# Turning the tokens of seven experts with VectorE blocks in place of TensorE transposes, in a fused attention and mixture-of-experts kernel

## The chip, the core and the metric

The kernel runs on one core of one Trainium2 chip. The metric is the device time of one launch in microseconds. The kernel before takes 764.63 us (median of 3 runs, 764.2 to 764.87).

## The reference

Bucketed attention over 4 batches of 8 heads, 768 tokens each, width 64, feeds a mixture of 8 experts that takes one expert per token:

```
mask   = q_bucket[:, :, :, None] == k_bucket[:, :, None, :]
attn   = softmax(where(mask, scale * q @ k.T, -1e9))
x      = (attn @ v).transpose(0, 2, 1, 3).reshape(3072, 512)
expert = argmax(x @ w_gate); gate_w = softmax(x @ w_gate)[expert]
for e in range(8):                      # tokens sorted by expert
    h = maximum(x_sorted[lo:hi] @ w1[e], 0)       # 512 -> 1024
    y_sorted[lo:hi] = h @ w2[e]                   # 1024 -> 512
out = gate_w * y (in the tokens' own order)
```

## The kernel before

The first 455 us or so are attention. Its results are scattered as rows of 578 floats into a table in device memory, `sorted_rows`, one stretch per expert: eight heads' 64 values with gate columns between them, then the gate weight and the token's number. The change does not touch that part, nor the first expert, which is taken in two halves of 256 tokens.

The rest is nine phases (`PH`). Phases 0 and 1 are the two halves of the fullest expert. Phases 2 to 8 are the seven others, in order of their fill, with room for 456, 432, 408, 396, 384, 372 and 354 tokens (`CAPS`). Phases 2 to 5 so have four row tiles of up to 128 tokens, phases 6 to 8 three.

In phase n, `mm1` (L697) makes the hidden values, 1024 of them in 8 groups of 128, each group 12 matmuls that move the tokens `xh` (feature on the partition, token along the free axis). Numbers are held as a rounded high part and a low part (a product is high x high and the two mixed ones), so the 4 chunks of 128 features need 3 matmuls each. ScalarE writes the high part of the relu (L711), VectorE the low part (L713). `mm2` makes the output: for phases of more than 384 tokens with features on the partitions (L734, 4 groups of 24), evicted as `yt` by ScalarE (L738) and turned back during the next phase's `mm1` (L763); for phases of up to 384 tokens by token (`yout`, L754, one group of 24 per row tile). VectorE applies the gate (L765), GpSimd scatters the rows (L767).

The tokens of phase n+1 are fetched by `rows(n + 1)` at the start of phase n: one DMA per row tile on SP's queue, 128 whole rows (L639, tile `xg`). During `mm2` of phase n they are turned by `xt` (L659): TensorE transposes each 128x128 block against an identity matrix into PSUM, ScalarE writes the high part of `xh` (L664), VectorE the low part (L665). A written table, `XT`, says behind or in the middle of which group of `mm2` each of the four chunks is turned. The gate weights and token numbers are copied by L662 and L645.

Weights: SP loads `raw` half chunks (L611), ScalarE writes the high part (L624), GpSimd the low part (L625), one phase ahead of their use, into six buffers; `halves` spreads those pieces over the groups of `mm1` and `mm2`. Each engine runs its instructions in the order in which they are written.

Of the kernel before, what the change touches and what calls it, by code (L numbers as in the profile page):

```python
# [7 lines left out]
F32 = mybir.dt.float32  # L8
F32R = mybir.dt.float32r
BF16 = mybir.dt.bfloat16  # L10
I32 = mybir.dt.int32
AF = mybir.ActivationFunctionType
OP = mybir.AluOpType
AX = mybir.AxisListType

B, H, S, D = 4, 8, 768, 64
# [5 lines left out]
DM = H * D  # L22
N = B * S
E = 8
F = 1024
PW = 2 * (D + E)
GC = NP * PW
RW = GC + 2
# [10 lines left out]
EARLY = 256  # L39
CAPS = [512, 456, 432, 408, 396, 384, 372, 354]  # L40
# [7 lines left out]
def tiles_of(n):  # L48

    return [(o, min(128, n - o)) for o in range(0, n, 128)]  # L50


@with_exitstack
def lsh_attention_moe(ctx, tc, qk, qk2, v, proj, wg, w1, w2, out):
    nc = tc.nc
    const = ctx.enter_context(tc.tile_pool(name="const", bufs=1))
    moe = ctx.enter_context(tc.tile_pool(name="moe", bufs=1))
# [3 lines left out]
    wk = attn.enter_context(tc.tile_pool(name="wk", bufs=2))  # L61
# [399 lines left out]
    EV = {}  # L461
# [133 lines left out]
    P2 = {}  # L595

    def raw_load(c, a):

        r, k = divmod(c, 4)
        if k < 2:  # L600
            src = w1[bass.ds(EV[r], 1)].rearrange("o (a p) f -> p (o a) f", p=128)[:, 2 * a:2 * a + 2,
                                                                                k * 512:(k + 1) * 512]
        else:
            o = (k - 2) * 4 + 2 * a
            src = w2[bass.ds(EV[r], 1)].rearrange("o (a p) d -> p (o a) d", p=128)[:, o:o + 2, :]
        n = 2 * c + a
        if n < 10 or n % 2:
            t = moe.tile([128, 2, 512], F32, name="raw", bufs=2)
        else:
            t = P2["p"].tile([128, 2, 512], F32, name="raw2", bufs=2)  # L610
        nc.sync.dma_start(t, src)  # L611
        RAW[c, a] = t
# [16 lines left out]
    PH = [(0, 0, EARLY), (0, EARLY, CAPS[0] - EARLY)] + [(r, 0, CAPS[r]) for r in range(1, E)]  # L629
    XG, IX, XH, HH, YT, GT = {}, {}, {}, {}, {}, {}  # L630
    outs = []
    xsv = xs.rearrange("(e c) w -> e c w", e=E)

    def rows(n):

        r, o, c = PH[n]
        XG[n] = wk.tile([128, 2, RW], F32, name="xd") if n < 2 else P2["p"].tile([128, 4, RW], F32, name="xg", bufs=2)
        for j, (i, _) in enumerate(tiles_of(c)):
            nc.sync.dma_start(XG[n][:, j], xsv[bass.ds(EV[r], 1), o + i:o + i + 128].rearrange("o p w -> p (o w)"))  # L639

    def tokens(n):
        r, o, c = PH[n]
        IX[n] = moe.tile([128, 4], I32, name="ix", bufs=3)
        t = len(tiles_of(c))
        nc.vector.tensor_copy(IX[n][:, :t], XG[n][:, :t, GC + 1].bitcast(I32))  # L645

    def heads(x, d):

        return x[:, d * PW + E:d * PW + E + 2 * D]

    def xt(n, d):
        r, o, c = PH[n]
        if d == 0:
            XH[n] = (moe.tile([128, 2, 4, EARLY], F32R, name="xhe") if n < 2 else
                     P2["p"].tile([128, 2, 4, CAPS[1]], F32R, name="xh"))
        p = ps.tile([128, 512], F32, name="t", bufs=2)
        t = len(tiles_of(c))
        for j in range(t):
            nc.tensor.transpose(p[:, j * 128:(j + 1) * 128], heads(XG[n][:, j], d), ident)  # L659
        if d == 0:  # L660
            GT[n] = moe.tile([128, 4], F32, name="gate", bufs=3)
            nc.vector.tensor_copy(GT[n][:, :t], XG[n][:, :t, GC])  # L662
            tokens(n)
        nc.scalar.activation(XH[n][:, 0, d, :c], p[:, :c], AF.Copy)  # L664
        nc.vector.tensor_tensor(XH[n][:, 1, d, :c], p[:, :c], XH[n][:, 0, d, :c], op=OP.subtract)  # L665
# [49 lines left out]
    def by_token(n):  # L715
        return PH[n][2] <= 384

    def mm2(n, m, mid=None):

        r, o, c = PH[n]  # L720
        if by_token(n):
            yout(n, m, mid)
            return
        if m == 0:
            YT[n] = (wk.tile([128, 4, EARLY], F32, name="qk") if n == 0 else
                     P2["p"].tile([128, 4, CAPS[1]], F32, name="yt"))
        h = HH[n]
        ms = slice(m * 128, (m + 1) * 128)
        p = ps.tile([128, 512], F32, name="s", bufs=3)
        k = 0  # L730
        for f in range(8):
            w = CH[4 * r + 2 + f // 4]
            for a, b in ((0, 0), (0, 1), (1, 0)):
                nc.tensor.matmul(p[:, :c], w[:, a, f % 4, ms], h[b][:, f, :c], start=(k == 0), stop=(k == 23))  # L734
                k += 1
                if k == 12 and mid:
                    mid()
        nc.scalar.activation(YT[n][:, m, :c], p[:, :c], AF.Copy)  # L738

    def yout(n, j, mid=None):  # L740
        r, o, c = PH[n]
        if j >= len(tiles_of(c)):
            return
        i, pw = tiles_of(c)[j]
        if n + 1 == len(PH) and j + 1 == len(tiles_of(c)):
            youts(n, j, i, pw)
            return
        p = ps.tile([128, 512], F32, name="s", bufs=3)
        if by_token(n):
            k = 0  # L750
            for f in range(8):
                w = CH[4 * r + 2 + f // 4]
                for a, b in ((0, 0), (1, 0), (0, 1)):
                    nc.tensor.matmul(p[:pw], HH[n][b][:, f, i:i + pw], w[:, a, f % 4],  # L754
                                     start=(k == 0), stop=(k == 23))
                    k += 1
                    if k == (12 if n else 20) and mid:
                        mid()
        else:

            yw = max(pw, min(128, CAPS[1] - i))
            for m in range(4):
                nc.tensor.transpose(p[:yw, m * 128:(m + 1) * 128], YT[n][:, m, i:i + yw], ident)  # L763
        y = (P2["p"] if n else moe).tile([128, DM], F32, name="y" if n else "ye", bufs=3 if n else 2)
        nc.vector.tensor_scalar(y[:pw], p[:pw], GT[n][:pw, j:j + 1], None, op0=OP.mult)  # L765
        nc.gpsimd.memset(C["spacer"], 0.0)
        st = nc.gpsimd.indirect_dma_start(out=out, out_offset=bass.IndirectOffsetOnAxis(ap=IX[n][:pw, j:j + 1], axis=0),  # L767
                                          in_=y[:pw], in_offset=None, bounds_check=N - 1, oob_is_err=False)
        for q in outs:
            tc.declare_no_dep(st.ins, q.ins, reason="rows of other tokens")  # L770
        outs.append(st)
# [222 lines left out]
    last = [route(B - 1, (0,)), route(B - 1, (1,))]  # L994
    for g in range(NG):
        for w in HEAD if g == 0 else LAST if g == NG - 1 else PLAN:
# [7 lines left out]
            if g == NG - 1 and w == "R9":  # L1004
                GT[0] = moe.tile([128, 4], F32, name="gate", bufs=3)
                nc.vector.tensor_copy(GT[0][:, :2], XG[0][:, :, GC])
                tokens(0)
    rows(1)
    rank_all()
    raw_load(4, 0)  # L1010
    raw_load(4, 1)
    def xts(n, ds):
        for d in ds:
            xt(n, d)
# [11 lines left out]
    def halves(n, k):  # L1026

        if n < 4 * E:
            chunk_part(n + k // 4, k % 4)
            if k % 2:  # L1030
                h = 2 * n + k // 2 + 3
                if h < LASTH:
                    raw_load(h // 2, h % 2)


    XT = {2: (((), (0, 1)), ((2,), (3,)), ((), ()), ((), ())),
          3: (((), (0,)), ((1,), (2,)), ((3,), ()), ((), ())),
          4: (((), (0,)), ((), (1,)), ((2,), (3,)), ((), ()))}
    raw_load(5, 0)
    plan = spill_plan()  # L1040
    for n in range(1, len(PH)):
        c0 = 4 * (PH[n][0] + 1)
        last = n + 1 == len(PH)
        if not last:
            rows(n + 1)
        for f in range(8):
            mm1(n, f)
            if f % 2 and not by_token(n - 1):
                yout(n - 1, f // 2)
            halves(c0, f)  # L1050
            if 3 <= n < 6:
                for _ in range(2):
                    next(plan, None)
        for m in range(4):
            mid, end = ((), ()) if last else XT[len(tiles_of(PH[n][2]))][m]
            if not (last and m == 3):
                mm2(n, m, lambda: xts(n + 1, mid))
            halves(c0 + 2, 2 * m)
            halves(c0 + 2, 2 * m + 1)
            xts(n + 1, end)  # L1060
        if n == 6:
            for _ in plan:
                pass
        if n == 7:
            C["n"] = nc.values_load(C["cntn"][0:1, 0:1], min_val=0, max_val=TMAX)
# [4 lines left out]
    with tc.If(C["n"] > 0):  # L1070
        with tc.For_i(0, C["n"], 1) as i:
# [16 lines left out]
            p = ps.tile([128, 512], F32, name="t", bufs=2)  # L1088
# [5 lines left out]
            for f in range(8):  # L1094
                p = ps.tile([128, 512], F32, name="t", bufs=2)
# [3 lines left out]
            p = ps.tile([128, 512], F32, name="s", bufs=3)  # L1099
# [31 lines left out]
```

## Time and profile before

| | |
|---|---|
| median of 3 runs | 764.63 us |
| the profiled execution | 764.64 us, of which the span 762.9 us |
| TensorE busy | 99% |
| VectorE, ScalarE, GpSimd busy | 56%, 63%, 61% |
| TensorE's granted clock | 0.998 of full |

The span is the time from the first to the last instruction on the core; the rest of the execution, 1.74 us, lies around it. Busy shares are averages over the attention part and the experts. The page's line of slices shows TensorE at 9 (90% or more) in every slice but the last. The duration of one matmul in the profile is the time from its start to its modelled end; matmuls overlap, so what one costs is read from the distance between starts.

### The profile page before, as it was taken

Reading aid. Unit: us, or ns where it says so; the run is one execution under the profiler, and the core shown is the slowest. Engines: PE = TensorE matmul, PEld = TensorE weight load, DVE = VectorE, ACT = ScalarE, POOL = GpSimd, SP = SyncE. Lnnn points to the kernel's source line nnn. Section 1 sums busy time; section 2 is a strip of 40 time slices with the busy share of each in tenths; the row PEclk is TensorE's granted clock in tenths of the full one; section 3 lists DMA queues with packets and bytes.
Section 4 is the critical chain, followed back from the end, with each engine's and each line's share of the span. In section 5 each row is a group of like instructions: output and inputs, shape, how many; then the busy total and the mean of one; then the engine's idle time right before and its main releaser. Section 6 shows DMA issues by size and latency. Waiting matters only on the chain.

```text
span 762.9 us, 13521 instructions
## 1 busy us (share of the span) xinstructions
PE 756.2 (99%) x4823; PEld 626.1 (82%) x4823; DVE 427.2 (56%) x1014; ACT 481.3 (63%) x942; POOL 467.3 (61%) x575
## 2 busy tenths in 40 slices
PE   9999999999999999999999999999999999999997
PEld 5778777777887777778788788899999999989896
DVE  8767766676676776767698673322545522232221
ACT  7878878887887887888788742444434344434320
POOL 6867445668635766754786464584655656668532
PEclk9999999999999999999999999999999999999999
DMA  8499825236323444530533235662545466545301
GB/s 286 162 310 285 293 97 166 95 120 213 127 68 138 128 155 144 166 106 21 166 130 120 84 103 195 236 220 96 179 129 181 141 113 200 178 145 188 104 10 37
DMA packets 48373, 115.12 MB, mean 151 GB/s; under 512 B 8867, under 2 KB 12707, under 8 KB 48304
## 3 DMA queue, kind: packets, MB, share of 16 engines
q1 hardware_dynamic: 41472, 97.88, 39.3%
q0 software_dynamic: 6688, 16.35, 6.4%
q8 instruction: 38, 0.62, 0.3%
q14 instruction: 31, 0.25, 0.1%
q10 hardware_dynamic: 144, 0.02, 0.0%
HBM read 88.39 MB, written 26.33 MB: 150 GB/s over the span
## 4 chain that ended last, share of the span: by engine, by line
PE 94%; issue 3%; POOL 1%; ACT 0%; DVE 0%; POOLq 0%; ACTq 0%
PE t L319 17%; PE s L697 17%; PE t L355 17%; PE s L734 10%; PE s L287 9%; PE s L285 9%; PE s L754 7%; PE t L374 3%; PE t L659 2%; PE t L243 2%; PE s L763 1%; POOL w L625 1%; PE t L105 1%; PE t L221 0%; POOL out_dram L767 0%
## 5 line engine op out<-in xcount | busy, mean ns | idle before, releaser
L295 DVE TENSOR_REDUCE m<-s 128x1 f32<-128x768 f32 x192 | 182.8, 952 | 95.2 <-PE s L287 86.0
L305 ACT ACTIVATE e<-s,m 128x768 f32<-128x768 f32 x192 | 190.9, 994 | 16.7 <-DVE m L297 9.8
L625 POOL TENSOR_TENSOR w<-raw,w 128x512 fp32r<-128x512 f32 x112 | 142.0, 1294 | 46.4 <-ACT w L624 45.8
L319 PE MATMUL t<-ident,e 128*128 128x128 f32 x1152 | 160.6, 275 | 0.6 <-ACT e L305 0.4
L345 ACT ACTIVATE pt<-t 128x512 f32<-128x512 f32 (+1 forms) x253 | 142.6, 592 | 29.2 <-PE t L319 26.0
L319 PEld LDWEIGHTS t<-ident,e 128*128 128x128 f32 x1152 | 132.6, 140 | 34.2 <-issue 12.6
L355 PE MATMUL t<-pt,vt 128*64 128x384 f32 x768 | 130.9, 490 | 0.0
L697 PE MATMUL s<-xh,w 128*128 128x456 f32 (+6 forms) x672 | 126.8, 346 | 0.0
L697 PEld LDWEIGHTS s<-xh,w 128*128 128x128 f32 x672 | 119.1, 188 | 2.9
L355 PEld LDWEIGHTS t<-pt,vt 128*64 128x64 f32 x768 | 52.3, 137 | 62.2 <-issue 60.1
L713 DVE SCALAR_TENSOR_TENSOR hh<-s,hh 128x256 fp32r<-128x256 f32 (+7 forms) x64 | 35.5, 555 | 91.8 <-ACT hh L711 91.8
L711 ACT ACTIVATE hh<-s 128x256 fp32r<-128x256 f32 (+7 forms) x64 | 31.3, 489 | 76.9 <-PE s L697 76.9
L734 PE MATMUL s<-hh,w 128*128 128x456 f32 (+3 forms) x384 | 78.7, 358 | 0.0
L734 PEld LDWEIGHTS s<-hh,w 128*128 128x128 f32 x384 | 69.9, 188 | 2.4
L624 ACT ACTIVATE w<-raw 128x512 fp32r<-128x512 f32 x112 | 66.3, 623 | 2.1 <-DMA raw<-in_w_dram 2.1
L767 POOL DMA_INDIRECT out_dram<-y,ix x26 | 25.9, 995 | 67.0 <-DVE y L765 34.6
L754 PE MATMUL s<-w,hh 128*128 128x512 f32 (+1 forms) x240 | 58.9, 398 | 0.0
L285 PE MATMUL s<-w 80*128 80x384 f32 x192 | 57.0, 378 | 0.0
L285 PE MATMUL s<-qk 80*128 80x384 f32 x192 | 56.3, 375 | 0.0
L665 DVE TENSOR_TENSOR xh<-t,xh 128x456 fp32r<-128x456 f32 (+6 forms) x28 | 16.0, 574 | 64.3 <-ACT xh L664 64.1
L754 PEld LDWEIGHTS s<-w,hh 128*128 128x128 f32 (+1 forms) x240 | 43.9, 187 | 9.5
L287 PE MATMUL s<-qk 128*128 128x384 f32 x192 | 50.1, 342 | 0.0
(203 smaller groups left out, 1016.8 us busy)
## 6 DMA issues: line engine op xcount, KB each, us to landing
raw<-in_w_dram SPq DMA_DIRECT2D x64, 512.0 KB, 3.7
xd<-in_qk_dram SPq DMA_DIRECT2D x16, 768.0 KB, 4.3
xhe<-in_qk_dram SPq DMA_DIRECT2D x15, 768.0 KB, 7.6
w<-in_qk_dram SPq DMA_DIRECT2D x14, 768.0 KB, 4.7
sorted_rows<-xr SPq DMA_DIRECT2D x8, 1156.0 KB, 14.5
xg<-sorted_rows SPq DMA_DIRECT2D x25, 289.0 KB, 5.2
vt<-in_v_dram SPq DMA_DIRECT2D x16, 384.0 KB, 4.0
masks<-bits SPq DMA_DIRECT2D x15, 192.0 KB, 1.9
```

The costliest lines, as they stand in the source:

```text
L285: nc.tensor.matmul(p[:, a, :HALF], k[0:80, 2, c], k[0:80, 3, n], start=i >= 4, stop=i < 4)
L287: nc.tensor.matmul(p[:, a, :HALF], k[:, 0, c], k[:, 1, n], start=i < 4, stop=i >= 4)
L295: nc.vector.tensor_reduce(m[:, 0:1], p[:, :, :HALF], axis=AX.XY, op=OP.max)
L305: nc.scalar.activation(e, p[:, :, :HALF], AF.Exp, bias=m[:, 2:3], scale=m[:, 1:2], accum_out=SM[g, hf][:, t, s:s + 1])
L319: nc.tensor.transpose(p[:, x * 128:(x + 1) * 128], e[w][:, kt // 3, (kt % 3) * 128:(kt % 3) * 128 + 128], ident)
L345: nc.scalar.activation(o, x, AF.Copy)
L355: nc.tensor.matmul(p[s * 64:(s + 1) * 64, :HALF], VT[g][:, kt, s, :], PT[u][:, s, kt, :], start=(kt == 0), stop=(kt == NT - 1))
L624: nc.scalar.activation(w[:, 0, a], r, AF.Copy)
L625: nc.gpsimd.tensor_tensor(w[:, 1, a], r, w[:, 0, a], op=OP.subtract)
L697: nc.tensor.matmul(p[:, :c], w[:, a, d, fs], x[:, b, d, :c], start=(k == 0), stop=(k == 11))
L734: nc.tensor.matmul(p[:, :c], w[:, a, f % 4, ms], h[b][:, f, :c], start=(k == 0), stop=(k == 23))
L754: nc.tensor.matmul(p[:pw], HH[n][b][:, f, i:i + pw], w[:, a, f % 4], start=(k == 0), stop=(k == 23))
```

## The change

For phases 2 to 8 the transposes on TensorE go. `rows` now fetches the tokens with four DMAs, one for each quarter of the partitions: partition 32a + i holds tokens i, 32 + i, 64 + i, ... and of each the 128 values of head pair a (tile `xb`, pieces of 512 bytes). A fifth DMA fetches gate and number (8 bytes per token) into the now small `xg`. VectorE turns each 32x32 block within its quarter (`xt_blocks`, tile `xt`), so partition 32a + r of chunk k holds feature 128a + 32k + r. ScalarE and VectorE write high and low part as before, now from `xt` in SBUF. w1 lies a second time in device memory with its rows in that order, and experts after the first read it there. The table `XT` is replaced by a rule: chunks 0 and 1 ahead of `mm2`'s first group, the others ahead of its second, or of its second and third.

```diff
@@ raw_load
-            src = w1[bass.ds(EV[r], 1)]...
+            src = (w1p if r else w1)[bass.ds(EV[r], 1)]...
@@ rows(n)
+        if n >= 2:
+            b = -(-c // 32)
+            x = XB[n] = P2["p"].tile([128, CB, 4 * 32], F32, name="xb")
+            for a in range(4):
+                nc.sync.dma_start(x[32 * a:32 * a + 32, :b],
+                                  xsv[bass.ds(EV[r], 1), o:o + 32 * b, a * PW + E:a * PW + E + 2 * D]
+                                  .rearrange("o (b i) w -> i (o b) w", i=32))
+            t = len(tiles_of(c))
+            XG[n] = P2["p"].tile([128, 4, 2], F32, name="xg", bufs=2)
+            nc.sync.dma_start(XG[n][:, :t], xsv[bass.ds(EV[r], 1), o:o + 128 * t, GC:GC + 2]
+                              .rearrange("o (j p) w -> p (o j) w", p=128))
+            return
@@ new
+    def xt_blocks(n, ks):
+        r, o, c = PH[n]
+        b = -(-c // 32)
+        if 0 in ks:
+            XH[n] = P2["p"].tile([128, 2, 4, CAPS[1]], F32R, name="xh")
+            XB[n] = XB[n], P2["p"].tile([128, 4, CB * 32], F32, name="xt")
+            t = len(tiles_of(c))
+            GT[n] = moe.tile([128, 4], F32, name="gate", bufs=3)
+            nc.vector.tensor_copy(GT[n][:, :t], XG[n][:, :t, 0])
+            tokens(n)
+        x, z = XB[n]
+        for k in ks:
+            nc.vector.transpose(z[:, k, :32 * b].rearrange("p (b i) -> p b i", i=32), x[:, :b, 32 * k:32 * k + 32])
+            nc.scalar.activation(XH[n][:, 0, k, :c], z[:, k, :c], AF.Copy)
+        for k in ks:
+            nc.vector.tensor_tensor(XH[n][:, 1, k, :c], z[:, k, :c], XH[n][:, 0, k, :c], op=OP.subtract)
@@ the phases
         for m in range(4):
-            mid, end = ((), ()) if last else XT[len(tiles_of(PH[n][2]))][m]
+            if not last:
+                xt_blocks(n + 1, ((0, 1), (2,), (3,), ())[m] if not by_token(n) else ((0, 1), (2, 3), (), ())[m])
             if not (last and m == 3):
-                mm2(n, m, lambda: xts(n + 1, mid))
+                mm2(n, m)
             halves(c0 + 2, 2 * m)
             halves(c0 + 2, 2 * m + 1)
-            xts(n + 1, end)
@@ host
+    w1 = np.asarray(inputs["moe_w1"]).reshape(E, 4, 4, 32, F).transpose(0, 2, 1, 3, 4)
+    w1 = np.ascontiguousarray(w1).reshape(E, DM, F)
```

TensorE, around the transposes of phase 2's tokens in `mm2` of phase 1 (`hh` are phase 1's hidden values, `w` its weights, `xg` phase 2's tokens), before:

```order
L754 MATMUL s<-w_5646,hh_5991 128x512
L659 MATMUL t<-ident,xg 128x128 x8
L754 MATMUL s<-w_5536,hh_5990 128x512 x2
...
L754 MATMUL s<-w_5536,hh_5991 128x512
L659 MATMUL t<-ident,xg 128x128 x4
L754 MATMUL s<-w_5646,hh_5990 128x512 x2
...
L659 MATMUL t<-ident,xg 128x128 x4
L697 MATMUL s<-xh,w_6007 128x456 x48
```

And now (L786 is the former L754, L729 the former L697):

```order
L786 MATMUL s<-w_5646,hh_5993 128x512
L786 MATMUL s<-w_5536,hh_5992 128x512 x2
...
L786 MATMUL s<-w_5536,hh_5993 128x512
L786 MATMUL s<-w_5646,hh_5992 128x512 x2
...
L786 MATMUL s<-w_5646,hh_5993 128x512
L729 MATMUL s<-xh,w_6009 128x456 x48
```

The 16 transposes are gone and the matmuls around them stand next to each other.

VectorE in the same phase, from the last low parts of `mm1`'s hidden values on, before:

```order
L713 SCALAR_TENSOR_TENSOR hh_5991<-s,hh_5990 128x256 x8
L765 TENSOR_SCALAR y<-s,gate 128x512
L662 COPY gate<-xg 128x4
L645 COPY ix<-xg 128x4
L665 TENSOR_TENSOR xh<-t,xh 128x456 x3
L765 TENSOR_SCALAR y<-s,gate 128x512
L665 TENSOR_TENSOR xh<-t,xh 128x456
```

And now:

```order
L745 SCALAR_TENSOR_TENSOR hh_5993<-s,hh_5992 128x256 x8
L675 COPY gate<-xg 128x4
L657 COPY ix<-xg 128x4
L679 STREAM_TRANSPOSE xt<-xb 128x480 x2
L682 TENSOR_TENSOR xh<-xt,xh 128x456 x2
L797 TENSOR_SCALAR y<-s,gate 128x512
L679 STREAM_TRANSPOSE xt<-xb 128x480 x2
L682 TENSOR_TENSOR xh<-xt,xh 128x456 x2
L797 TENSOR_SCALAR y<-s,gate 128x512
```

The first half of the turning now stands ahead of the eviction of `mm2`'s first group (L797, the former L765), the second half ahead of that of the last.

SP's queue at the start of phase 1, before:

```order
L611 DMA raw_5983<-in_w_dram 128x2x512 [waits DMASW6_49,DMASW7_49,DVE_49,DMAHW5_49,PE_49,DMAHW6_49,Activation_49,Pool_49]
L639 ISA
L639 DMA xg<-sorted_rows 128x578
...
L611 DMA raw<-in_w_dram 128x2x512 [waits DMAHW7_49,Pool_49]
L611 ISA
L611 DMA raw_6063<-in_w_dram 128x2x512
```

And now (`in_w1p` is the second w1):

```order
L611 DMA raw_5983<-in_w1p_dram 128x2x512 [waits DMASW6_49,DMASW7_49,DVE_49,DMAHW5_49,PE_49,DMAHW6_49,Activation_49,Pool_49]
L641 ISA
L641 DMA xb<-sorted_rows 32x15x128
...
L646 DMA xg<-sorted_rows 128x4x2
L611 ISA
L611 DMA raw<-in_w1p_dram 128x2x512 [waits DMAHW7_49,Pool_49]
L611 ISA
L611 DMA raw_6065<-in_w_dram 128x2x512 [waits DMAHW0_49]
```

Between the same two loads of `raw` there were four loads of rows, and there are now four quarters and one small one.

## Rows read from the trace of the kernel before

**Rows 1.** The page: TensorE's busy time; chain by engine; the row loads, KB and landing.
```profile
PE 756.2 (99%) x4823; PEld 626.1 (82%) x4823; DVE 427.2 (56%) x1014; ACT 481.3 (63%) x942; POOL 467.3 (61%) x575
...
PE 94%; issue 3%; POOL 1%; ACT 0%; DVE 0%; POOLq 0%; ACTq 0%
...
xg<-sorted_rows SPq DMA_DIRECT2D x25, 289.0 KB, 5.2
```
**Rows 2.** Windows, phases 1, 7: length, busy PE, PEld, DVE, ACT, POOL, clock, DMA.
```profile
471.00:495.00 24.00, 24.00 (x158) 21.74 (x157) 6.97 (x17) 10.87 (x24) 14.72 (x14) 1.00 0.73 262
...
691.00:725.00 34.00, 34.00 (x181) 30.49 (x180) 8.80 (x17) 13.79 (x29) 23.25 (x22) 1.00 0.45 155
```
**Rows 3.** Instructions of tile xg: duration ns min/median/max, first and last start.
```profile
L659 PE MATMUL t<-ident,xg x100: 270/272/273, 487.5 to 722.5; 128*128 128x128 f32 x100
```
**Rows 4.** Timeline of TensorE, phase 4: start us, us, line, operands, count.
```profile
577.54 4.66 PE L697 MATMUL s<-xh,w 128*128 128x408 f32 x24
582.03 0.60 PE L763 MATMUL s<-ident,yt 128*128 128x128 f32 x4
582.39 4.74 PE L697 MATMUL s<-xh,w 128*128 128x408 f32 x24
586.97 0.60 PE L763 MATMUL s<-ident,yt 128*128 128x128 f32 x4
...
597.18 4.72 PE L734 MATMUL s<-hh,w 128*128 128x408 f32 x24
601.75 0.60 PE L659 MATMUL t<-ident,xg 128*128 128x128 f32 x4
602.10 4.71 PE L734 MATMUL s<-hh,w 128*128 128x408 f32 x24
...
616.88 4.48 PE L697 MATMUL s<-xh,w 128*128 128x396 f32 x24
```
**Rows 5.** Timeline of TensorE, mm2 of phase 1, to the next mm1.
```profile
481.92 5.72 PE L754 MATMUL s<-w,hh 128*128 128x512 f32 x24
487.48 1.04 PE L659 MATMUL t<-ident,xg 128*128 128x128 f32 x8
...
494.72 20.22 PE L697 MATMUL s<-xh,w 128*128 128x456 f32 x96
```
**Rows 6.** Timeline of TensorE, mm2 of phase 6, first group.
```profile
673.05 5.80 PE L754 MATMUL s<-w,hh 128*128 128x512 f32 x24
678.69 0.49 PE L659 MATMUL t<-ident,xg 128*128 128x128 f32 x3
678.93 3.05 PE L754 MATMUL s<-w,hh 128*128 128x512 f32 x12
```
**Rows 7.** Groups by line, 471 to 763 us: busy us, mean ns; idle before.
```profile
L625 POOL TENSOR_TENSOR w<-raw,w 128x512 fp32r<-128x512 f32 x112 | 142.0, 1294 | 46.4 <-ACT w L624 45.8
...
L765 DVE TENSOR_SCALAR y<-s,gate 128x512 f32<-128x512 f32 (+5 forms) x26 | 19.3, 743 | 30.4 <-PE s L754 30.4
L665 DVE TENSOR_TENSOR xh<-t,xh 128x456 fp32r<-128x456 f32 (+6 forms) x28 | 16.0, 574 | 64.3 <-ACT xh L664 64.1
...
L555 DVE TENSOR_TENSOR le<-le,spl 128x192 f32<-128x192 f32 x1 | 1.5, 1458 | 0.0
```
**Rows 8.** Timeline of SP's queue at the start of phase 1.
```profile
471.32 2.26 SPq L639 DMA_DIRECT2D xg<-sorted_rows  x4
476.33 25.73 SPq L611 DMA_DIRECT2D raw<-in_w_dram  x8
```
**Rows 9.** Timeline of all engines, end of phase 1's mm1: its last low part.
```profile
482.65 0.63 ACT L624 ACTIVATE w<-raw 128x512 fp32r<-128x512 f32 x1 [1.58 <-DMA raw<-in_w_dram]
...
483.59 0.43 DVE L713 SCALAR_TENSOR_TENSOR hh<-s,hh 128x256 fp32r<-128x256 f32 x1 [2.06 <-ACT hh L711]
```
**Rows 10.** DMA, 471 to 484 us: packets, bytes and rate.
```profile
DMA packets 2300, 4.64 MB, mean 357 GB/s; under 512 B 175, under 2 KB 175, under 8 KB 2298
```
**Rows 11.** DMA, 622 to 626 us (the spill table's store): queue, packets, MB, share.
```profile
q1 hardware_dynamic: 2784, 0.06, 98.0%
```

More of the change, by code (lines that the diff above doesn't have):

```diff
@@ L53, in lsh_attention_moe @@
 @with_exitstack
-def lsh_attention_moe(ctx, tc, qk, qk2, v, proj, wg, w1, w2, out):
+def lsh_attention_moe(ctx, tc, qk, qk2, v, proj, wg, w1, w1p, w2, out):
     nc = tc.nc
@@ L600, in raw_load @@
         if k < 2:
-            src = w1[bass.ds(EV[r], 1)].rearrange("o (a p) f -> p (o a) f", p=128)[:, 2 * a:2 * a + 2,
+            src = (w1p if r else w1)[bass.ds(EV[r], 1)].rearrange("o (a p) f -> p (o a) f", p=128)[:, 2 * a:2 * a + 2,
                                                                                 k * 512:(k + 1) * 512]
@@ L636, in rows @@
         r, o, c = PH[n]
-        XG[n] = wk.tile([128, 2, RW], F32, name="xd") if n < 2 else P2["p"].tile([128, 4, RW], F32, name="xg", bufs=2)
+        if n >= 2:
[10 more added lines that the diff above has]
+            return
+        XG[n] = wk.tile([128, 2, RW], F32, name="xd")
         for j, (i, _) in enumerate(tiles_of(c)):
@@ L644, in tokens @@
         t = len(tiles_of(c))
-        nc.vector.tensor_copy(IX[n][:, :t], XG[n][:, :t, GC + 1].bitcast(I32))
+        nc.vector.tensor_copy(IX[n][:, :t], XG[n][:, :t, XG[n].shape[2] - 1].bitcast(I32))
     def heads(x, d):
         return x[:, d * PW + E:d * PW + E + 2 * D]
+    CB = -(-CAPS[1] // 32)
+    XB = {}
+    def xt_blocks(n, ks):
[14 more added lines that the diff above has]
+            nc.vector.tensor_tensor(XH[n][:, 1, k, :c], z[:, k, :c], XH[n][:, 0, k, :c], op=OP.subtract)
     def xt(n, d):
@@ L653, in xt @@
         if d == 0:
-            XH[n] = (moe.tile([128, 2, 4, EARLY], F32R, name="xhe") if n < 2 else
-                     P2["p"].tile([128, 2, 4, CAPS[1]], F32R, name="xh"))
+            XH[n] = moe.tile([128, 2, 4, EARLY], F32R, name="xhe")
         p = ps.tile([128, 512], F32, name="t", bufs=2)
@@ L1033, in halves @@
                     raw_load(h // 2, h % 2)
-    XT = {2: (((), (0, 1)), ((2,), (3,)), ((), ()), ((), ())),
-          3: (((), (0,)), ((1,), (2,)), ((3,), ()), ((), ())),
-          4: (((), (0,)), ((), (1,)), ((2,), (3,)), ((), ()))}
     raw_load(5, 0)
@@ L1120 @@
         wg[s, :, :, s * E:s * E + E] = np.asarray(inputs["moe_w_gate"]).reshape(NP, 2, D, E)[:, s].transpose(1, 0, 2)
+    w1 = np.asarray(inputs["moe_w1"]).reshape(E, 4, 4, 32, F).transpose(0, 2, 1, 3, 4)
+    w1 = np.ascontiguousarray(w1).reshape(E, DM, F)
     pj, wg = pj.reshape(2 * D, 32), wg.reshape(2 * D, NP, 2 * E)
     arrays = {"in_qk_dram": qk, "in_qk2_dram": np.concatenate([qk, qk], 1), "in_v_dram": vv, "in_proj_dram": pj, "in_wg_dram": wg,
-              "in_w1_dram": np.ascontiguousarray(inputs["moe_w1"]), "in_w2_dram": np.ascontiguousarray(inputs["moe_w2"])}
+              "in_w1_dram": np.ascontiguousarray(inputs["moe_w1"]), "in_w1p_dram": w1,
+              "in_w2_dram": np.ascontiguousarray(inputs["moe_w2"])}
     nc = bacc.Bacc("TRN2", target_bir_lowering=False, num_devices=1, dynamic_dma_scratch_size=2048)
```

## The prediction

> **What bounds the kernel now.** I read the page first: TensorE is busy for 756.2 of 762.9 us, and the chain that ended last runs through it for 94% [rows 1]. An average can hide stages with other limits, so the busy time by stretch comes next: in phases 1 and 7 TensorE is busy for all of the 24.00 and 34.00 us, at the full granted clock, while VectorE works 6.97 and 8.80 us of them, ScalarE 10.87 and 13.79, GpSimd 14.72 and 23.25 [rows 2]. So in the phases that the change touches every nanosecond on TensorE's queue counts, and the other engines have room. Then the instructions to be removed: 100 transposes of `xg` on TensorE [rows 3]. Their 272 ns each is a time from start to modelled end and overlaps the neighbours, so it isn't the price; that is read from starts in TensorE's timeline.
>
> **What the removal is worth.** Phase 4 shows a piece with and without interruption. Its `mm1` group of 24 with no transposes ahead lasts from 577.54 to 582.03, 4.49 us; the next, just behind four transposes, from 582.39 to 586.97, 4.58: an interruption also slows what follows it by 0.09. In `mm2` the four transposes of `xg` start at 601.75 and the next matmul at 602.10: 0.35. The whole `mm2` of phase 4 runs from 597.18 to 616.88, 19.70 us, for 96 matmuls of the same width [rows 4]. Without the transposes of `xg` it would be 4 x 4.49 = 17.96, and 0.09 for those of `yt` that stay ahead of it, 18.05. Saved: 1.65 us for 16 transposes, 0.103 each.
>
> Phase 1 has other matmuls: 24 of them from 481.92 to 487.48, 5.56 us, the whole `mm2` of 48 and 16 transposes up to 494.72, 12.80 [rows 5]. 12.80 - 2 x 5.56 = 1.68, 0.105 each.
>
> With three row tiles an interruption is three transposes: 678.69 to 678.93, 0.24 [rows 6], and with the 0.09 behind it 0.33, 0.110 each. The 5.64 us of the group ahead of it (673.05 to 678.69), which itself follows transposes, is 5.56 + 0.08, so the 0.09 holds here too.
>
> Phases 2 to 5 have 4 x 16 = 64 transposes, phases 6 to 8 3 x 12 = 36, together the 100 of [rows 3]. 64 x 0.104 + 36 x 0.110 = 6.66 + 3.96 = 10.6 us, all of it on the path that sets the end.
>
> **What is added, and what hides it.** VectorE: per phase four block transposes of up to 480 columns. No row shows one. From below I take 480 columns at the pace of the subtraction L665 (574 ns for some 400 to 456, [rows 7]), 0.6 us; from above the pace of L555, 192 elements in 1.458 us [rows 7], 3.6 us. I take 0.6, since L665 is the nearer in shape and on the same data. The four subtractions (574 ns) and ScalarE's four copies of the same size only change their source from PSUM to SBUF; for one of either I take 0.6 again, between 0.4 (a faster read) and L555's 1.458. VectorE's sum rises by 2.4 us in a phase of 24 to 41: hidden by its idle time, as long as the tokens are turned in time.
>
> In time means before `mm1` of the next phase. Phase 1 is the tightest. Its `mm2` would run from 481.92 to 493.0 (2 x 5.56). The low part of the last relu ends at 484.0 [rows 9]; 0.3 for gate and numbers, two transposes and two subtractions, 1.2 each pair, take VectorE to 486.7. Chunks 2 and 3 stand behind the eviction of the first group (0.743, L765 in [rows 7]), which begins at 487.5: done at 488.2, two transposes to 489.4, a copy to 490.0, two subtractions to 491.2. The first group of `mm1` wants the last low part as its 11th matmul, some 2 us after 493.0. So 3.8 us are spare. In the other phases `mm2` is 17 to 18 us long and more is spare. What stands behind the turning on ScalarE (`yt`, the weights' high parts) and on VectorE (`y`) waits for it at most as long; weights are made one phase ahead and cost nothing by that.
>
> Loads: phase 1 again. The row loads are issued from 471.32 on [rows 8]; a typical one lands after 5.2 us [rows 1], and the turning needs it only from about 482.5. But the `raw` load issued behind them at 476.33 [rows 8] is one for which ScalarE already waits 1.58 us, until 482.65 [rows 9]; behind that wait stands the relu of the last group, which TensorE needs for the last 3 of the first 24 matmuls of `mm2`, at 481.92 + 21 x 0.232 = 486.8. The low part of that relu is done at 484.0 [rows 9], so 2.8 us are spare. Four loads of 289 KB [rows 1] are 1.18 MB, at the 357 GB/s of that stretch [rows 10] 3.3 us. Now 480 x 4 pieces of 512 bytes, 0.98 MB, and 512 of 8 bytes. By bytes alone 2.8 us, earlier by 0.5. By pieces: a store of 8-byte pieces shows 2784 in 4 us at 98% busy [rows 11], 1.44 ns each; 2432 of them would be 3.5 us, and if that comes on top of the bytes, 6.3, later by 3.0. So the stall lies between 0 and 0.2 us; I take 0. Twice the price of a piece would make it 3.7. Later phases give the loads more time: phase 4's `mm1` lasts 19.6 us (577.54 to 597.18, [rows 4]).
>
> The Trainium skill, "DMA: Bandwidth & Descriptors", Specifications, asks at least 512 bytes for full rate. By it the tokens' pieces run at full rate and only the 512 small ones suffer, so the sum is that by bytes. No row here shows a piece of 512 bytes.
>
> SP issues 5 DMAs for 4 or 3; the four take 2.26 us [rows 8], so 0.6 to 1.1 more per phase, ahead of a load due later: 0, with a loss of the same size where that isn't so, inside the 2.8. The second w1 is read in the same pieces from another place: 0.
>
> **Sum.** The profiled execution took 764.64 us, the median of runs 764.63, so no correction: 764.64 - 10.6 = 754.0 us.
>
> **Rivals.** *A: only the starts count.* The 0.09 behind each interruption might belong to something that stays (the change of PSUM buffer). Then 64 x 0.088 + 36 x 0.08 = 8.5 us go: 756.1. Against it: `mm1` pays it behind `yt`'s transposes and not without them [rows 4].
>
> *B: the load behind the quarters is late in phase 1.* Pieces at twice the price above: a stall of 3.7 us once, 757.7. For it: ScalarE waits there already, and the quarters are untried; against it: the bytes fall by a sixth.
>
> *C: no gain, because GpSimd's low parts of the weights set the pace.* They take 1.294 us each [rows 7], 16 in a phase. Phase 7 has 23.25 us of GpSimd in 34.00 [rows 2]; shortened to 32.7 it keeps 9 us of room. The time would be 764.6 only if that work grew by 40%.
>
> *D: slower, because the tokens are turned late.* If VectorE's instructions on two SBUF operands and its block transposes take what L555 shows rather than L665, the chain decides. Then a block transpose takes 3.6 us and a subtraction 1.46. In phase 1, from 484.3 on, two of each take VectorE to 494.4, past the eviction's 487.5; eviction, two transposes, a copy and two subtractions end at 494.4 + 0.7 + 7.2 + 0.6 + 2.9 = 505.8, against 495.0 wanted: a wait of 10.8 us. In each of the other six the same work, 0.8 + 14.4 + 0.6 + 5.8 and an eviction, is 22 us against 17 to 18 us of `mm2` and 2 of grace: some 2.5, in all 15. 764.6 - 10.6 + 10.8 + 15 = 779.8. It decides from where the transposes alone, the rest at 0.6, take more than 2 us each (phase 1 begins to wait), and the gain is eaten up near 3.9. For it: L555's 1.458 us for 192 elements shows that an instruction of VectorE with its operands in SBUF can take several times its work while GpSimd runs. Against it: that row is one, and most of such a delay would be a wait of one GpSimd instruction (1.294), not a rate.
>
> The Trainium skill, "SBUF — State Buffer", Summary: rules for kernel authors, speaks for D: a VectorE instruction with two SBUF inputs and a GpSimd one that reads SBUF exclude each other, and the later one stands still until the other ends. L555's row agrees with it. By it each of the 28 subtractions, now with both inputs in SBUF, may wait up to 1.294 us: in phase 1 the first two slip by 2.6 us, which moves the eviction by 1.8, and the last two by 2.6 more: 4.4 against the 3.8 that are spare, so 754.6; and GpSimd loses at most 28 x 0.574 = 16 us over seven phases, which its room holds.
>
> **How the numbers follow.** Chances: forecast 0.80, A 0.06, B 0.05, C 0.03, D 0.06. A difference of under 0.2% (1.5 us) can't be told from none. The forecast alone spans 752.8 to 755.5 (0.09 or 0.12 behind each interruption, a stall of up to 1.2 us). The range takes in A and B: 752.6 to 757.8. Faster is the forecast, A and B, 0.91; same C, 0.03; slower D, 0.06.
>
> **What would show it.** In the new profile the 96 or 72 matmuls of `mm2` stand without a gap: phase 4's in 18.0 to 18.1 us, phase 1's in 11.1. TensorE's busy share stays at 99%, its count falls by 100. The block transposes take about 0.6 us, the first of phase 1 starts right behind the last low part of `mm1`, and the `raw` load behind the quarters lands before 485.5. A gap on TensorE at the start of an `mm1`, ended by `xh`, would show D; one near the end of phase 1's first `mm2` group, ended by `hh`, B. The forecast is wrong if TensorE waits anywhere for `xh` or `hh`, or if `mm2`'s groups keep their 0.09.

## The result and the profile after

The changed kernel takes 755.38 us (median of 4 runs, 754.94 to 757.27) against 764.43 for the kernel before beside it: ratio 0.9886, 95% interval [0.9868, 0.9904]. In a later set of runs, with the first experiments below, it took 754.14 against 764.69, ratio 0.9855 [0.9838, 0.9871]. The forecast was 754.0, the range 752.6 to 757.8.

The page of the changed kernel, busy time by engine and the chain by engine:

```profile
PE 745.7 (99%) x4723; PEld 616.2 (82%) x4723; DVE 456.5 (61%) x1042; ACT 483.2 (64%) x942; POOL 470.5 (62%) x575
...
PE 90%; issue 3%; DMA 2%; POOL 1%; DVE 1%; ACT 1%; POOLq 0%; DVEq 0%; SPq 0%; ACTq 0%
```

Against [rows 1], TensorE has 100 instructions and 10.5 us less and is still the bound. But the chain, 94% TensorE before, now gives 2% to a DMA and 1% to VectorE: something other than TensorE is late somewhere. TensorE's timeline, from phase 1's `mm2` on, shows where (in brackets: idle time, and what ended it):

```profile
481.78 5.03 PE L786 MATMUL s<-w,hh 128*128 128x512 f32 x21
487.65 6.52 PE L786 MATMUL s<-w,hh 128*128 128x512 f32 x27 [0.84 <-ACT hh L743]
494.01 1.61 PE L729 MATMUL s<-xh,w 128*128 128x456 f32 x7
496.28 18.80 PE L729 MATMUL s<-xh,w 128*128 128x456 f32 x89 [0.66 <-DVE xh L682]
514.92 19.99 PE L766 MATMUL s<-hh,w 128*128 128x456 f32 x96
534.75 4.87 PE L729 MATMUL s<-xh,w 128*128 128x432 f32 x24
...
593.88 18.17 PE L766 MATMUL s<-hh,w 128*128 128x408 f32 x96
611.88 4.48 PE L729 MATMUL s<-xh,w 128*128 128x396 f32 x24
...
666.75 16.91 PE L786 MATMUL s<-w,hh 128*128 128x512 f32 x72
683.49 16.37 PE L729 MATMUL s<-xh,w 128*128 128x372 f32 x96
```

Two waits, both at phase 1: behind the 21st matmul of `mm2` (487.65), for the last relu's values, and behind the 7th of the next `mm1` (496.28), for the tokens. In the six phases after it nothing waits. Phase 4's `mm2`, 19.70 us in [rows 4], lasts 18.00 (593.88 to 611.88).

In all eleven profiles, those of the experiments included, phase 0's first `mm1` begins at 454.71 to 454.89 us, but phase 1's at 469.73 to 472.30: the executions differ by up to 2.6 us in phase 0. So I compare profiles from the start of phase 1's `mm1` to the start of phase 8's `mm2`. Phase by phase, in us, from starts in the timelines of single profiled executions:

| stretch | before | changed | saved |
|---|---|---|---|
| `mm2` of phase 1 | 12.80 | 12.23 | 0.57 |
| `mm1` of phase 2 | 20.06 | 20.91 | -0.85 |
| `mm2` of phase 2 | 21.53 | 19.83 | 1.70 |
| `mm2` of phase 3 | 20.73 | 18.98 | 1.75 |
| `mm2` of phase 4 | 19.70 | 18.00 | 1.70 |
| `mm2` of phase 5 | 18.71 | 17.42 | 1.29 |
| `mm2` of phase 6 | 18.13 | 16.74 | 1.39 |
| `mm2` of phase 7 | 17.99 | 16.73 | 1.26 |
| whole | 270.65 | 261.86 | 8.79 |

The 84 transposes of phases 2 to 7 gave 9.09 us, 0.108 each. Those of phase 1 gave nothing in this execution: with the next `mm1`, 0.28 us was lost there.

What happened there, first on SP's queue (start, duration of the issue), to be read against [rows 8]:

```profile
471.42 4.19 SPq L641 DMA_DIRECT2D xb<-sorted_rows  x4
475.81 2.93 SPq L646 DMA_DIRECT2D xg<-sorted_rows  x1
479.00 1.54 SPq L611 DMA_DIRECT2D raw<-in_w1p_dram  x1
```

The four loads of rows were issued within 2.26 us and the `raw` load behind them at 476.33. Now the five take until 478.74, and the `raw` load goes out at 479.00. ScalarE, which needs it (against [rows 9]):

```profile
486.70 0.63 ACT L624 ACTIVATE w<-raw 128x512 fp32r<-128x512 f32 x1 [5.35 <-DMA raw<-in_w1p_dram]
```

It waits 5.35 us in place of 1.58, and starts that copy 4.05 us later than before. Of these 2.8 us were spare; the relu behind it is what TensorE waits for. That is rival B's place, at a smaller size than its 3.7 us.

VectorE, which could begin the turning only behind that relu's low part, and GpSimd beside it:

```profile
488.70 1.23 DVE L679 STREAM_TRANSPOSE xt<-xb 128x480 f32<-128x480 f32 x2
490.02 1.20 DVE L682 TENSOR_TENSOR xh<-xt,xh 128x456 fp32r<-128x456 f32 x2
491.13 0.75 DVE L797 TENSOR_SCALAR y<-s,gate 128x512 f32<-128x512 f32 x1
491.79 1.23 DVE L679 STREAM_TRANSPOSE xt<-xb 128x480 f32<-128x480 f32 x2
493.12 3.65 DVE L682 TENSOR_TENSOR xh<-xt,xh 128x456 fp32r<-128x456 f32 x2
```
```profile
493.18 2.55 POOL L625 TENSOR_TENSOR w<-raw,w 128x512 fp32r<-128x512 f32 x2
```

The first two subtractions take 1.20 us together. The second two begin with two of GpSimd's weight pieces, take 3.65 us, and the first of them ends only when both pieces are done (at 495.73):

```profile
493.12 3.11 DVE L682 TENSOR_TENSOR xh<-xt,xh 128x456 fp32r<-128x456 f32 x1
```

From 470 us to the end (busy us, mean ns, against L665 in [rows 7]):

```profile
L682 DVE TENSOR_TENSOR xh<-xt,xh 128x456 fp32r<-128x456 f32 (+6 forms) x28 | 30.5, 1117 | 15.5 <-ACT xh L680 15.1
...
L679 DVE STREAM_TRANSPOSE xt<-xb 128x384 f32<-128x384 f32 (+3 forms) x28 | 15.7, 587 | 0.0
```

The subtraction, with the same arithmetic, takes 1117 ns in place of 574 in the mean. The block transpose takes the 0.6 us that was assumed.

### The profile page after: what moved, and what is told of

Same layout as the page of the kernel before. It is cut to its first block, busy times and chain, and to the rows that moved or that the text cites. A ratio compares the mean times of both kernels' runs of the same rounds, so it can differ in the third digit from the quotient of the medians.

```text
span 753.9 us, 13381 instructions
## 1 busy us (share of the span) xinstructions
PE 745.7 (99%) x4723; PEld 616.2 (82%) x4723; DVE 456.5 (61%) x1042; ACT 483.2 (64%) x942; POOL 470.5 (62%) x575
## 4 chain that ended last, share of the span: by engine, by line
PE 90%; issue 3%; DMA 2%; POOL 1%; DVE 1%; ACT 1%; POOLq 0%; DVEq 0%; SPq 0%; ACTq 0%
PE t L319 17%; PE t L355 17%; PE s L729 15%; PE s L766 10%; PE s L287 9%; PE s L285 9%; PE s L786 6%; PE t L374 3%; DMA raw<-in_w1p_dram 2%; PE t L243 2%; PE s L795 1%; POOL w L625 1%; PE t L105 1%; DVE xh L682 1%; ACT e L305 0%
## 5 line engine op out<-in xcount | busy, mean ns | idle before, releaser
L625 POOL TENSOR_TENSOR w<-raw,w 128x512 fp32r<-128x512 f32 x112 | 144.6, 1317 | 39.7 <-ACT w L624 39.1
L729 PE MATMUL s<-xh,w 128*128 128x456 f32 (+6 forms) x672 | 127.0, 346 | 0.7 <-DVE xh L682 0.7
L729 PEld LDWEIGHTS s<-xh,w 128*128 128x128 f32 x672 | 119.1, 188 | 4.1 <-DVE xh L682 1.0
L766 PE MATMUL s<-hh,w 128*128 128x456 f32 (+3 forms) x384 | 74.9, 355 | 0.0
L786 PE MATMUL s<-w,hh 128*128 128x512 f32 (+1 forms) x240 | 56.7, 395 | 0.8 <-ACT hh L743 0.8
L786 PEld LDWEIGHTS s<-w,hh 128*128 128x128 f32 (+1 forms) x240 | 44.5, 187 | 11.7 <-ACT hh L743 1.3
L253 POOL TENSOR_SCALAR bits<-bits,wsg 64x384 f32<-64x384 f32 x15 | 18.7, 1245 | 50.2 <-ACT bits L226 50.2
```

The lines of the kernel that those rows point to most:

```text
L625: nc.gpsimd.tensor_tensor(w[:, 1, a], r, w[:, 0, a], op=OP.subtract)
L729: nc.tensor.matmul(p[:, :c], w[:, a, d, fs], x[:, b, d, :c], start=(k == 0), stop=(k == 11))
```

## The experiments

Theory 1: TensorE saves about 0.108 us for each transpose, and in phase 1 two late things take it back, the `raw` load behind the quarters and the subtractions beside GpSimd. The rivals say in each case what else could make those waits. "The whole" below is the stretch of the table above.

**The changed kernel again.** No edit.

> The changed kernel as it is, beside the variants that follow. Theory: TensorE saves 0.103 to 0.110 us for each of 100 transposes, 10.6 us in all, and loses about 1.9 of it in and just after phase 1, where the raw load behind the quarters lands late (0.84 us of wait for hh) and the last low parts of xh come late (0.66 us of wait for xh). So 755.4 again, both waits of the same size. Rival: the waits are chance of one execution; then one of them is missing here, and the time is 754.

Measured: 754.14 us (753.39 to 755.04), ratio 0.9855 [0.9838, 0.9871]; the whole 261.30. The wait for the tokens is there again (0.67 us); the one for the relu is 0.28, not 0.84. So the wait for the tokens has the same size in both executions, and the one for the relu varies. The medians of the two sets of this kernel, 755.38 and 754.14, lie 1.2 us apart, and the execution profiled here is the slowest of its set (755.04): what the two waits cost is known for the profiled executions alone.

**The raw load first.**

```diff
-        if n < 10 or n % 2:
+        if n != 11 and (n < 10 or n % 2 or n == 12):
...
-                if h < LASTH:
+                if h < LASTH and h != 11:
...
     raw_load(5, 0)
+    raw_load(5, 1)
```

> The one raw load that phase 1 wants soonest (second half of chunk 5) is issued ahead of the row loads, into the buffer that the next one used. Theory: it lands by about 475 instead of 486; the wait for hh (0.84 us) goes, VectorE starts the turning about 3.5 us earlier, so the wait for xh (0.66 us) goes too if the quarters, 512 KB later in the queue, land by 485: 753.9, phase 1's mm2 in 11.2 us. Rival: the quarters themselves are late and the wait only moves to xh: 755 to 756, with the block transposes of phase 1 waiting for a DMA.

Measured: 753.72 us (753.66 to 753.91), ratio 0.9853 [0.9836, 0.9869]; the whole 259.82, 10.83 less than before. TensorE's timeline has no wait left:

```profile
481.78 11.28 PE L786 MATMUL s<-w,hh 128*128 128x512 f32 x48
492.90 20.16 PE L729 MATMUL s<-xh,w 128*128 128x456 f32 x96
```

Phase 1's `mm2` takes 11.12 us. So without the late `raw` load neither wait is there. VectorE now waits for the loads instead:

```profile
486.26 0.17 DVE L675 COPY gate<-xg 128x4 f32<-128x4 f32 x1 [3.43 <-DMA xg<-sorted_rows]
...
490.86 3.68 DVE L682 TENSOR_TENSOR xh<-xt,xh 128x456 fp32r<-128x456 f32 x2
```

The small load, last of the five, lands at 486.26, and the long subtractions are still there; they end at 494.5, just in time. Its whole is 1.48 us shorter than that of the changed kernel beside it (259.82 against 261.30). The medians differ by 0.4 us, less than the runs of the changed kernel scatter, so that it beats the changed kernel is shown by the profile and not by the times.

**Phase 2's tokens on TensorE as before, the others by blocks.**

```diff
-            src = (w1p if r else w1)
+            src = (w1p if r > 1 else w1)
...
+            if n == 2:
+                XG[n] = x
+                for j, (i, _) in enumerate(tiles_of(c)):
+                    nc.sync.dma_start(x[:, j], xsv[bass.ds(EV[r], 1), o + i:o + i + 128].rearrange("o p w -> p (o w)"))
+                return
...
-            if not last:
+            mid, end = (((), (0, 1)), ((2,), (3,)), ((), ()), ((), ()))[m] if n == 1 else ((), ())
+            if not last and n > 1:
                 xt_blocks(n + 1, ((0, 1), (2,), (3,), ())[m] if not by_token(n) else ((0, 1), (2, 3), (), ())[m])
-                mm2(n, m)
+                mm2(n, m, lambda: xts(n + 1, mid))
...
+            xts(n + 1, end)
```

> Phase 2's tokens are loaded as whole rows and turned by TensorE as before; phases 3 to 8 by blocks. Theory: phase 1's mm2 takes its old 12.8 us, no wait there, the later six phases keep their saving of 84 transposes (1.70, 1.75, 1.70, 1.29, 1.39 and 1.26 us, 9.1 in all): 764.4 - 9.1 = 755.3, the same as the changed kernel, whose phase 1 gained nothing. Rival: the two waits of phase 1 don't come from the quarters and block transposes: they stay, 756.8.

Measured: 755.40 us (754.94 to 755.64), ratio 0.9872 [0.9856, 0.9889]; the whole 261.53, 9.12 less than before. Phase 1's `mm2` takes 12.81 us and TensorE waits nowhere. The theory's 755.3 is met: in the profiled executions (261.53 against 261.86 and 261.30) the part of the change that concerns phase 1 brings nothing beyond 0.3 us either way. By the medians of this set, 755.40 against 754.14, it would bring 1.3; those carry the scatter of phase 0, so this stays open.

**No quarter loads.** The tokens of phases 2 to 8 are a constant tile.

```diff
-            x = XB[n] = P2["p"].tile([128, CB, 4 * 32], F32, name="xb")
-            for a in range(4):
+            if "xb" not in C:
+                C["xb"] = P2["p"].tile([128, CB, 4 * 32], F32, name="xb")
+                nc.vector.memset(C["xb"], 0.01)
+            x = XB[n] = C["xb"]
+            for a in ():
```

> The quarter loads are left out: the tokens of phases 2 to 8 are a constant tile, turned and multiplied as in the changed kernel (the output is not the reference's). The small load of gate and number stays. Theory: the pieces of 512 bytes are what made the raw load late; without them SP issues it at 476.3, it lands by 480, no wait for hh or xh: 753.8. Rival: the wait comes from the small load or from SP's fifth issue: half or more of it stays, 754.6 or more.

Measured: 753.72 us (753.62 to 754.24), ratio 0.9854 [0.9838, 0.9871]; the whole 259.84, no wait. The quarters are what delayed the `raw` load; the small load is still in this kernel and costs nothing. SP's four issues went with the quarters, so this run does not tell their transfer from their issue.

**The subtraction with one operand in PSUM.** The low part of the tokens is computed from a zeroed tile.

```diff
+        if "zp" not in C:
+            C["zp"] = ps.tile([128, 512], F32, name="t", bufs=2)
+            nc.vector.memset(C["zp"], 0.0)
...
-            nc.vector.tensor_tensor(XH[n][:, 1, k, :c], z[:, k, :c], XH[n][:, 0, k, :c], op=OP.subtract)
+            nc.vector.tensor_tensor(XH[n][:, 1, k, :c], C["zp"][:, :c], XH[n][:, 0, k, :c], op=OP.subtract)
```

> In the changed kernel the low part of xh takes a zeroed tile in PSUM in place of the block-turned tile in SBUF (the output is not the reference's), so the subtraction has one operand in SBUF, as it had before the change. Theory: the subtraction grew because with both operands in SBUF it stands still while GpSimd's weight pieces run; it falls from a mean near 1.1 us (longest 3.2) back to 0.55 to 0.6, none over 0.7, and the wait for xh at the start of phase 2's mm1 (0.67 us) goes; the wait for hh stays: 753.5 to 754.5, 0.7 less than the changed kernel. Rival: the long subtractions come from the turned tile being late or from ScalarE; they stay long, and the wait for xh too.

Measured: 753.96 us (753.63 to 754.96), ratio 0.9859 [0.9842, 0.9877]; the whole 259.84. Its subtraction and GpSimd's weight pieces:

```profile
L625 POOL TENSOR_TENSOR w<-raw,w 128x512 fp32r<-128x512 f32 x112 | 142.3, 1296 | 41.1 <-ACT w L624 40.2
...
L685 DVE TENSOR_TENSOR xh<-t,xh 128x456 fp32r<-128x456 f32 (+6 forms) x28 | 15.2, 573 | 20.9 <-ACT xh L683 20.2 <-issue 0.2
```

573 ns, as before the change, and GpSimd's pieces 1296 in place of 1317. So the second operand in SBUF is what doubled the subtraction. In phase 1 the second two again begin 0.06 us ahead of two of GpSimd's pieces, and take 1.19 us in place of 3.65:

```profile
492.29 1.19 DVE L685 TENSOR_TENSOR xh<-t,xh 128x456 fp32r<-128x456 f32 x2
492.35 2.57 POOL L625 TENSOR_TENSOR w<-raw,w 128x512 fp32r<-128x512 f32 x2
```

The wait for the relu, which I expected to stay, is gone: in this execution the `raw` load went out at 477.35 and was used from 485.31, 14.62 us after the start of phase 1's `mm1` (16.55 and 15.97 in the two profiles of the changed kernel). The wait for the tokens is gone too, and an earlier start alone doesn't do that: with half pieces, below, the turning begins at the same place (17.26 us after that start, here 17.23), the subtractions are long, and TensorE waits 0.48 us. So that wait needs both, the late start and the long subtractions.

**Each block transpose three times,** on top of the version with the raw load first.

```diff
+            for _ in range(3):
                 nc.vector.transpose(z[:, k, :32 * b]..., x[:, :b, 32 * k:32 * k + 32])
```

> The version with the raw load first, with each block transpose done three times (1.8 us in place of 0.6). Theory: in phases 2 to 7 mm2 hides it wholly (their mm2 keep 19.83, 18.98, 18.00, 17.42, 16.74 and 16.73 us); only phase 1 is late: there VectorE starts at 486.3, so its last low part comes 4 x 1.2 = 4.8 us later than now, at 497 to 499.5, against 495 wanted, a wait of 2 to 4.5 us: 755.7 to 758.2. Rival: the turning has no room in the other phases either, 28 more of 1.2 us each or 4.8 us per phase show as waits for xh: above 760.

Measured: 756.36 us (756.02 to 756.60), ratio 0.9888 [0.9871, 0.9904]. One wait for the tokens, at phase 2's `mm1`:

```profile
493.53 2.02 PE L730 MATMUL s<-xh,w 128*128 128x456 f32 x7
496.96 18.95 PE L730 MATMUL s<-xh,w 128*128 128x456 f32 x89 [1.41 <-DVE xh L683]
515.75 4.49 PE L767 MATMUL s<-hh,w 128*128 128x456 f32 x21
```

That `mm1` takes 22.22 us in place of 19.99. The `mm2` of phases 2 to 7 keep their times to 0.01 us. So phases 2 to 7 hide 1.8 us for each block transpose, and phase 1 doesn't. VectorE's added work is smaller than that sounds: the transposes take 50.0 us in place of 15.7, but the subtractions, both operands still in SBUF, fall from 1118 to 664 ns in the mean, 12.1 us in all. What they cost depends on which of GpSimd's pieces they fall beside. Rival D put its threshold at 2 us, with the turning begun at 484.3; here it begins at 486.4, behind the loads, so the threshold is lower.

**Half pieces.** Each quarter as two loads with pieces of 256 bytes.

```diff
+              for s in (0, D):
-                nc.sync.dma_start(x[32 * a:32 * a + 32, :b], ...a * PW + E:a * PW + E + 2 * D]
+                nc.sync.dma_start(x[32 * a:32 * a + 32, :b, s:s + D], ...a * PW + E + s:a * PW + E + s + D]
```

> The changed kernel with each quarter loaded as two halves, pieces of 256 bytes in place of 512, twice as many, same bytes. Theory (a piece has its own price, 46 ns on each of 16 engines or 2.9 ns overall): the loads of phase 2's tokens take 5.6 us more, the raw load behind them lands that much later and the wait for hh grows from 0.3 to 0.8 to 5.5 to 6.5 us; the other phases have the room: 759.5 to 761.5. Rival (the bytes set the time of a load, 46 ns being what 512 bytes cost): the waits stay as they are, 754 to 755.5.

Measured: 755.76 us (755.16 to 756.06), ratio 0.9879 [0.9862, 0.9895]; the whole 260.56, a wait of 0.48 us for the tokens, none for the relu. My theory of a price per piece (759.5 to 761.5) fell: the whole is no longer than the changed kernel's. The median lies 0.3 us above the rival's range; in its profile phase 1 begins at 471.01, some 0.9 us later than in the changed kernel's two. The rate, in a stretch that holds almost only these pieces, first the changed kernel (478 to 481 us), then this one (the same stretch):

```profile
DMA packets 1093, 0.53 MB, mean 178 GB/s; under 512 B 81, under 2 KB 1088, under 8 KB 1093
```
```profile
DMA packets 1950, 0.48 MB, mean 161 GB/s; under 512 B 1950, under 2 KB 1950, under 8 KB 1950
```

The bytes go at half of the 357 GB/s of [rows 10] with either piece. That left the other thing that the quarters change: each DMA writes only 32 partitions.

**All partitions, and long pieces.** Two kernels take the two apart: the same pieces of 512 bytes, but each DMA over 128 partitions; and quarters with pieces of 2048 bytes. In both the tokens arrive in another order.

```diff
 # all partitions
-                nc.sync.dma_start(x[32 * a:32 * a + 32, :b], ...
+                nc.sync.dma_start(x[:, 4 * a:4 * a + 4], ... .rearrange("o (j p) w -> p (o j) w", p=128))
 # long pieces
+                nc.sync.dma_start(x[32 * a:32 * a + 32].rearrange("p (j b) w -> p j (b w)", j=4),
+                                  xsv[..., o + 128 * a:o + 128 * a + 128, E:E + 512].rearrange("o (j i) w -> i (o j) w", i=32))
```

> The same count of DMAs for each phase's tokens and the same pieces of 512 bytes (2048 of them in place of at most 1920), but each DMA writes all 128 partitions, four pieces to each, in place of 32 partitions with 15 pieces each (the tokens then lie in another order and the output is not the reference's). Theory Q: the quarter is what halves the rate (512 bytes take 46 ns on an engine, a whole row of 2312 bytes 94 ns); here the loads run at 300 GB/s or more, a piece takes about 25 ns, the four land in some 4 us, the raw load behind them lands before 484 and no wait for hh is left: 753.7 to 754.3. Theory P: the short piece is what costs; the rate stays near 180 GB/s and the raw load lands at 485 to 487 as in the changed kernel.

> Quarters as in the changed kernel, 32 partitions to a DMA, but in pieces of 2048 bytes, four to a partition (again another order of tokens, the output is not the reference's; 262 KB for 246 KB in a quarter). Theory Q (32 partitions at a time halve the rate): the rate stays near 180 GB/s, a piece takes some 180 ns on its engine against 84 for the raw loads' pieces of the same size, and the raw load behind them lands at 485 or later. Theory P (short pieces): 300 GB/s or more, the raw load lands before 484, 753.7 to 754.3.

Measured: 753.88 us (753.23 to 755.80), ratio 0.9862 [0.9845, 0.9878], the whole 259.82; and 753.54 (752.97 to 754.67), ratio 0.9862 [0.9846, 0.9879], the whole 260.16. The rate from 506 to 509 us, while phase 3's tokens come in, all partitions first:

```profile
DMA packets 1967, 0.89 MB, mean 297 GB/s; under 512 B 227, under 2 KB 1967, under 8 KB 1967
```
```profile
DMA packets 485, 0.63 MB, mean 211 GB/s; under 512 B 176, under 2 KB 176, under 8 KB 485
```

Short pieces over all partitions run at 297 GB/s; long pieces into a quarter at 211. In the same phase of the changed kernel, short pieces into quarters, from 507.4 to 510.4 us:

```profile
DMA packets 1150, 0.57 MB, mean 190 GB/s; under 512 B 38, under 2 KB 1150, under 8 KB 1150
```

The quarter is the larger part of the loss (297 against 190 with the same pieces), the piece the smaller (211 at 2048 bytes, 190 at 512, 162 at 256 in this phase). In landing times the two are less apart than I expected: counted from the start of phase 1's `mm1`, ScalarE got the `raw` load after 13.36 us with all partitions, 14.81 with long pieces, and 12.34 before the change. The loads of the changed kernel gave 16.55, 15.97 and 14.62 in three executions, so only the 13.36 lies clear of their scatter. Neither waits for the relu, but with long pieces phase 2's `mm1` still takes 20.31 us in place of 19.99.

Does the `raw` load come late because SP issues it late? Its issue, and ScalarE's copy of it, with all partitions and then with long pieces:

```profile
479.80 1.82 SPq L611 DMA_DIRECT2D raw<-in_w1p_dram  x1
485.66 0.63 ACT L624 ACTIVATE w<-raw 128x512 fp32r<-128x512 f32 x1 [2.60 <-DMA raw<-in_w1p_dram]
```
```profile
475.56 0.39 SPq L611 DMA_DIRECT2D raw<-in_w1p_dram  x1
484.54 0.63 ACT L624 ACTIVATE w<-raw 128x512 fp32r<-128x512 f32 x1 [4.04 <-DMA raw<-in_w1p_dram]
```

With long pieces it goes out 5.83 us after the start of that `mm1`, earlier than before the change (6.02), and is used 2.47 us later; with all partitions it goes out at 7.50 and is used earlier than with long pieces. How fast the bytes ahead of it move counts for more than when it is issued.

## Why the prediction was right, and where it was off

*What the removal is worth: right.* 10.6 us were forecast; where nothing is late the whole shrinks by 10.83 (raw load first) and 10.81 (no quarter loads). The method held at each step: prices from distances between starts, not the 272 ns of one transpose, and 0.09 us behind each interruption. Rival A, which left those 0.09 out (8.5 us), is excluded by the same two numbers, although by the time alone the first set's 755.38 lies nearer to its 756.1 than to 754.0.

*What hides VectorE's work: right for the transposes* (0.6 forecast, 0.587 measured), and for phases 2 to 7 with room to spare. *Wrong for the subtractions:* "only change their source from PSUM to SBUF", 0.6 us. They take 1.117. The rule of the Trainium skill, "SBUF — State Buffer", Summary: rules for kernel authors, was cited beside L555's 1.458 us and put under rival D; the one-operand run shows that it was a term of the forecast: 573 against 1117 ns with nothing else changed in the instruction. The trace agrees that one stands still while the other works, but not in the size: a subtraction was allowed one piece of GpSimd's (1.294 us), and the one at 493.12 stood still through two and took 3.11 us. That the price worked out for TensorE, 4.4 us of delay against 3.8 spare, comes out at 0.6 and the wait for the tokens at 0.66 is luck: the first two subtractions were not held up (1.20 us), the last two by 2.45, and TensorE waited only because the turning also began late. With the raw load first the last two take 3.68 us and nothing waits.

*The loads in phase 1: the step that failed.* I bounded the delay of the `raw` load at 3.0 us, "by bytes alone" -0.5 and "by pieces" from the 8-byte store, and took the stall as 0. It was used 4.05 us later than before. Both ends were about bytes at 357 GB/s and piece counts; what sets these loads' rate first is how many partitions one DMA writes (178 to 190 GB/s into quarters, 297 over all), which no row of before shows, and the end of the range should have been open there. SP's issues, taken as 0.6 to 1.1 us more, took 7.3 us in place of 2.26, and the `raw` load went out 2.67 us later. The stall of 0.2 us at most became 0.84 and 0.28 in two executions. By the prediction's own sign, that TensorE waits nowhere for `xh` or `hh`, the forecast fails in phase 1: it waited for both there, the `raw` load was used at 486.7 and not before 485.5, and phase 1's `mm2` took 12.23 us and not 11.1. The time stayed within the range because the loss was small, 1.5 to 2.0 us in the two profiles, not because the loads came in time. By the same mechanism rival B was half true: its place was right, its reason (twice the price of a piece) not, as the half pieces show.

*The sum.* 764.64 - 10.83 + 2.04 is 755.85 us; the profiled execution took 755.68. The 2.04 are 261.86 - 259.82, the whole of the changed kernel against that with the raw load first: the two waits of 0.84 and 0.66 us, and 0.54 more that the two stretches lost beside them; I did not part that further. In the second profile the same difference is 1.48 us.

*Rivals C and D.* GpSimd's pieces grew from 1294 to 1317 ns and never set the pace. D as a whole did not come: block transposes run at the pace of L665. Its place, phase 1's tokens, is where the second wait stands.

## What to carry to other kernels

When work leaves the bound engine, look for the one stage with the least room, here the shortest phase, and bound each new transfer and each changed operand there: the other six phases hid everything. A load that others queue behind is priced by its rate, and the rate by its destination too; if something urgent is behind it, issue that first (no wait left in that profile). And moving an operand from PSUM to SBUF is not free on VectorE while GpSimd works on SBUF.

## What the runs showed of the hardware

DMAs into 32 partitions each ran at 162, 190 and 211 GB/s with pieces of 256, 512 and 2048 bytes, nearly the same amount over 128 partitions in pieces of 512 bytes at 297, all while phase 3's tokens came in. The loads' issue on SP grew with the backlog too: the small load of 4 KB took 2.93 us to issue behind the quarters in phase 1, against 0.39 to 0.78 in the later phases. I did not test what SP waits for there.

A subtraction on VectorE with both operands in SBUF took 0.52 to 3.24 us (mean 1.117) in the phases where GpSimd makes its weight pieces; with one operand in PSUM it took 0.52 to 0.63 (mean 0.573). The block transposes, which read one operand, from SBUF, took 0.52 to 0.67 us in the same phases and show no such waits.
